# A list schedule ordered by one rank for each piece, in a block-sparse attention with a gated feed-forward layer

## The chip, the cores and the metric

The kernel runs on one core of one Trainium2 chip. The metric is the time of one execution on the device in microseconds (us), as the median of several runs. The core has five engines that run on their own and wait for each other by semaphores: TensorE (PE; PEld is its weight load), VectorE (DVE), ScalarE (ACT), GpSimd (POOL) and SyncE (SP). SP and POOL here also issue the transfers (DMAs): those of SP are on queue q1, those of POOL on queue q0.

## The reference

Attention of 4 batches, 8 heads, 768 positions in 24 blocks of 32, 64 wide, with a block mask; its output goes through a gated feed-forward layer ("expert" in the change's words; there is one).

```python
scores = scale * np.matmul(q, k.transpose(0, 1, 3, 2))
mask = np.abs(blk_i - blk_j) <= window          # the block itself and its two neighbours
mask = mask | (blk_i == 0) | (blk_j == 0) | (blk_i == n_blocks - 1) | (blk_j == n_blocks - 1)
for qb in range(n_blocks):
    for kb in sampled_blocks[qb]:               # three blocks given at run time
        mask[qb * block:(qb + 1) * block, kb * block:(kb + 1) * block] = True
attn = softmax(np.where(mask, scores, -1e9))
x = (attn @ v), heads side by side: (3072, 512)
gate = 1.0 / (1.0 + np.exp(-(x @ w_gate)))      # w_gate, w_val: (512, 1536)
out = (gate * (x @ w_val)) @ w_out              # w_out: (1536, 512)
```

## The kernel before

The kernel describes its work as about 1,100 pieces, each with a name, an engine (or a choice of two), an estimated duration, the pieces that it depends on, the buffers that it takes and gives back, and a priority. A planner (`Planner.run`, L197) then makes a list schedule when the kernel is built: again and again it takes, for each engine, among the pieces that could start soonest (within 0.2 us on TensorE, 0.02 on the others) the one with the lowest priority number, and appends it. The result is a fixed order of instructions on each engine. On the chip each engine works through its order, and an instruction that waits holds up all behind it.

The pieces of one batch b, by the start of their names:
- `ldv`, `ldk`, `ldq` (L559, L563): loads of V, K, Q with a cast to f16, on POOL's queue. The weights `wg`, `wv` in four quarters each and `wo` in three (L578, L586) are on the same queue. `GATES` (L37) lists weight loads that are let go only after a named V gather of batch 0 was issued, and `LGATE` (L40) does so for the loads of the next batch.
- `shk`, `shq` (L722): a rearrangement of the loaded K or Q in SBUF from heads to rows, on POOL or VectorE; `vsh` (L773) the same for V on VectorE, and `scr` (L782) writes it to DRAM.
- `trk`, `trq` (L743; L746 in batch 0): TensorE transposes, four for each; `evk`, `evq` (L756, L761, L763) take them out of PSUM to `KT` and `QT`, on VectorE or ScalarE.
- `kfl`, `kg` (L881, L870): gathers of the first, last and three sampled K blocks of a query block into `KG`, the latter on POOL.
- `w`, `vg` (L815, L894): gathers of V windows and sampled V blocks from DRAM, on SP. `vfl` (L799; L681 in batch 0) fetches V's first and last block to `FL`, and `vfc` (L827 on VectorE, L829 on POOL) copies them beside each window.
- For each of 11 steps of two query blocks: `sc` scores (L914, L921), `mx` row maximum (L930, VectorE), `ex` exponential (L942, ScalarE), `rz` reciprocal (L949), `sl` scaling (L965 on VectorE, L962 on ScalarE), `tp` transpose (L976, TensorE), `te` its copy (L982), `pv` product of P and V (L995), `xe` its copy to the layer's input `XA` (L1011, L1016). In batches 2 and 3 the scores of two steps are one piece.
- Four "dense" units for the first and last query block, which see all keys: `dsc` (L644), `dmx` (L1046), `dex` (L1052), `dsl` (L1060, L1061), `dtp` (L1070), `dte` (L1075), `dpv` (L1083), `dxe` (L1100).

The feed-forward layer works on seven groups of 256 or 512 positions (`GROUPS`), each of which can start when the attention of its positions is done. A group has 12 pieces, one for each 128 hidden columns: a gate half and a value half on TensorE (L1138, four matmuls each), a tanh on ScalarE (L1146) and a multiply on VectorE into `HT` (L1151). Then comes one output piece of 12 matmuls for each 128 positions (L1173), scaled into `YS` (L1180, L1182) and stored by SP (L1187). The output piece reads the 12 parts of `HT` in their order. While TensorE would stand in the first 60 us, the planner puts filler matmuls in (L1207).

What sets the order: attention pieces have a priority of 10 b plus 0.1 for each step, expert pieces 1000 + 100 g + f for part f of group g, so that attention goes first and expert pieces go by number. `OFFSETS` (L44) adds a small number for each kind of piece and batch, and for quarters of a batch (`kind`, L72; `third`, L83), in one loop before the planner runs (L1216 to L1218).

Of the kernel before, what the change touches and what calls it, by code (L numbers as in the profile page):

```python
# [33 lines left out]
PREP = [-50.0, 0.27, 10.34, 20.65]  # L34


GATES = {0: 4, 2: 7, 3: 7, 4: 9, 6: 5, 7: 7, 8: 6}  # L37


LGATE = {1: 10, 2: 11, 3: 2}  # L40

OFFSETS = {  # L44
    "dense1": 0.26, "dense2": 0.10, "dense3": 0.10, "evk0": -0.74, "evk1": -0.80, "evk2": -1.45, "evk3": -0.55,
    "evq0": 1.25, "evq1": 0.23, "evq2": -0.22, "evq3": -1.58, "ex0": 0.01, "ex0.d": -0.84, "ex1": -0.18,
    "ex1.b": -0.01, "ex1.c": -0.03, "ex1.d": 0.01, "ex2": -1.17, "ex2.c": 0.10, "ex3": -3.42, "ex3.a": -0.08,
    "ex3.d": -0.29, "kfl0": -0.91, "kfl1": -0.90, "kfl2": -0.39, "kfl3": -0.88, "kg0": -0.57, "kg0.a": 0.09,
    "kg1": 0.44, "kg1.d": 0.06, "kg2": 0.38, "kg3": 1.19, "kg3.c": 0.03, "ldk0": -0.43, "ldk1": -0.02, "ldk2": -0.35,
    "ldk3": 0.64, "ldq0": 0.85, "ldq1": 0.76, "ldq2": -0.07, "ldq3": -0.32, "ldv0": -0.29, "ldv1": 0.02,  # L50
    "ldv2": 0.03, "ldv3": -0.01, "mx0": -0.39, "mx1": 0.02, "mx1.c": -0.01, "mx2": 0.03, "mx3": 1.95, "mx3.d": 0.02,
    "pv0": 0.57, "pv1": 0.02, "pv1.b": 0.26, "pv1.c": 0.30, "pv1.d": 0.54, "pv2": -0.07, "pv2.a": 0.06, "pv3": 1.33,
    "pv3.c": -0.25, "rz0": -1.33, "rz0.b": 0.04, "rz0.c": 0.02, "rz1": 0.18, "rz1.b": -0.37, "rz1.d": 0.16,
    "rz2": -0.18, "rz2.c": 0.08, "rz2.d": -1.06, "rz3": -2.19, "rz3.a": 0.35, "rz3.c": -0.66, "sc0": -0.04,
    "sc0.c": 1.29, "sc0.d": 0.01, "sc1": -0.04, "sc1.a": 0.32, "sc2": -0.40, "sc2.b": 0.01, "sc3": 0.07,
    "sc3.a": 0.68, "scr0": 1.03, "scr1": 0.86, "scr2": -2.19, "scr3": 0.72, "shk1": 0.12, "shk2": -0.83,
    "shk3": 0.25, "shq1": 0.21, "shq2": 0.21, "shq3": 1.91, "sl0": -0.54, "sl0.c": 0.04, "sl1": -2.38, "sl2": -0.07,
    "sl2.a": 1.08, "sl2.c": -0.06, "sl2.d": -0.48, "sl3": 2.15, "te0": 0.19, "te0.a": 0.89, "te0.d": 0.03,
    "te1": 0.28, "te1.a": 0.82, "te1.b": 0.06, "te2": 0.03, "te3": -0.62, "te3.a": -0.57, "te3.c": -0.18,
    "tp0": 0.19, "tp0.a": -0.07, "tp1": -0.18, "tp1.c": 0.20, "tp1.d": 1.12, "tp2": 0.13, "tp2.d": -0.01,  # L60
    "tp3": 0.14, "tp3.b": 0.45, "trk0": -0.17, "trk1": 0.02, "trk2": -0.07, "trk3": -0.68, "trq0": -0.55,
    "trq1": -0.41, "trq2": -0.01, "trq3": 0.27, "vfc0": -0.46, "vfc1": -0.62, "vfc2": 0.03, "vfc3": -0.03,
    "vfl0": 1.61, "vfl1": -1.53, "vfl2": -0.18, "vfl3": 1.68, "vg0": -0.06, "vg1": -0.57, "vg1.d": 0.01, "vg2": 0.05,
    "vg3": 0.17, "vg3.b": 0.10, "vsh0": -0.45, "vsh1": 0.09, "vsh2": -0.22, "w0": 0.04, "w0.c": 1.86, "w1": -1.01,
    "w1.a": -0.04, "w1.d": -0.16, "w2": -0.63, "w2.c": 0.37, "w2.d": 0.08, "w3": 0.23, "w3.b": 0.03, "wg0": 0.97,
    "wg1": -0.05, "wg2": -0.51, "wg3": -0.04, "wo0": -0.07, "wo1": 0.62, "wo2": -0.30, "wv0": 0.24, "wv1": 1.00,
    "wv2": 0.32, "wv3": -1.88, "xe0": -0.31, "xe0.d": 0.33, "xe1": -1.46, "xe2": -0.10, "xe2.c": -0.61, "xe3": -0.01,
    "xe3.d": -0.01,
}


def kind(o):  # L72

    if o.prio <= -90 or o.prio >= 900:
        return None
    n = len(o.name) - len(o.name.lstrip("abcdefghijklmnopqrstuvwxyz"))
    c, b = o.name[:n] or "x", o.name.lstrip("abcdefghijklmnopqrstuvwxyzABCDEFGHIJKLMNOPQRSTUVWXYZ")[:1]
    if c in ("dsc", "dmx", "dex", "dsl", "dtp", "dte", "dpv", "dxe"):
        c = "dense"
    return c + (b if b.isdigit() else "x")  # L80


def third(o, k):  # L83

    n = o.name.split("_")
    x = n[1] if k is not None and len(n) > 1 and n[0].isalnum() and n[0][-1].isdigit() else ""
    d = x[: len(x) - len(x.lstrip("0123456789"))]
    return k + "." + "abcd"[min(int(d) // 6, 3)] if d and n[0][:-1].isalpha() else None


class Op:
# [264 lines left out]
def kernel(  # L356
# [145 lines left out]
    pl = Planner()  # L502
# [606 lines left out]
    for b in range(B):  # L1109
        lv = attention(b, 10.0 * b, prev)  # L1110
        for n, i in GATES.items() if b == 0 else ():
            FF["gate"][n].after.append(vgs[0, i])
        prev = [lv] + ([FF["w"]["wo", NF - 1]] if b == 0 else []) + ([vgs[b, LGATE[b + 1]]] if b < B - 1 else [])

# [6 lines left out]
    for g, G in enumerate(GROUPS):  # L1121
        n = 128 * len(G)
# [90 lines left out]
        return o  # L1213

    pl.fill = fill
    for o in pl.ops:  # L1216
        k = kind(o)
        o.prio += OFFSETS.get(k, 0.0) + OFFSETS.get(third(o, k), 0.0)  # L1218
    order = pl.run()
    PLAN.clear()  # L1220
    PLAN.extend((o.name, o.eng, o.start, o.end) for o in order)
# [36 lines left out]
```

## Time and profile before

| what | value |
|---|---|
| runs | 334.35 us median of 3 (333.45 to 334.68) |
| the profiled execution | 333.25 us; span from first to last instruction 331.5 us |
| mean granted TensorE clock | 0.995 |
| TensorE busy | 309.1 us (93%), of which fillers (L1207) 10.8 + 10.2 us |
| VectorE, ScalarE, POOL busy | 241.4, 219.1, 100.9 us |
| first expert matmul (L1138) | 44.6 us |
| q0: transfers of POOL | 16.39 MB |
| q1: transfers of SP | 24.83 MB |

A busy TensorE is not TensorE at its peak, as its matmuls overlap. Times of the order of work are from the start of the span. In the rows of a timeline stand start, length, engine, line, operation, what is written and read, how many instructions, and in brackets how long the engine stood before and what ended that. In the rows of stages stand the stage, its length, the busy time of PE, PEld, DVE, ACT and POOL with their instructions, the granted clock, the DMA share and GB/s.

### The profile page before, as it was taken

The numbers are of one execution on the slowest core, as the hardware profiler recorded it, in microseconds if no ns is written. First come the engines' busy times: TensorE is split into PE (matmuls) and PEld (weight loads), VectorE is DVE, ScalarE is ACT, GpSimd is POOL, SyncE is SP. The second block draws the span as 40 slices with busy tenths as digits, with TensorE's granted clock in tenths as the row PEclk, the third lists the DMA queues.
The fourth block names the chain that finished last, engine by engine and source line by source line (L and its number), as shares of the span: only waits on it lengthen the run. The fifth ranks groups of instructions, "written<-read, shape, count | busy, mean of one in ns | idle before, by whom it ended". The sixth has DMA issues, their size and how long they took to land.

```text
span 331.5 us, 12349 instructions
## 1 busy us (share of the span) xinstructions
PE 309.1 (93%) x4568; PEld 187.1 (56%) x4568; DVE 241.4 (73%) x542; ACT 219.1 (66%) x650; POOL 100.9 (30%) x332
## 2 busy tenths in 40 slices
PE   6998887998899799999999999999999999999996
PEld 2555566866766356655555655655655665444443
DVE  3399899936887979878898969999996577504310
ACT  1248889854597789766998566679995868423322
POOL 6499642036743632402330427022220010000000
PEclk9999999999999889999999999999999999999999
DMA  7959999979449862235389093531323400020002
GB/s 116 195 186 228 224 226 227 222 184 269 110 69 231 242 136 87 71 96 145 115 159 190 32 223 114 157 96 35 108 72 116 117 11 3 0 97 32 0 34 95
DMA packets 42063, 41.99 MB, mean 127 GB/s; under 512 B 6323, under 2 KB 38196, under 8 KB 42004
## 3 DMA queue, kind: packets, MB, share of 16 engines
q0 software_dynamic: 17376, 16.39, 30.0%
q1 hardware_dynamic: 24628, 24.83, 25.4%
q8 instruction: 36, 0.59, 0.8%
q14 instruction: 23, 0.19, 0.2%
HBM read 45.97 MB, written 9.44 MB: 167 GB/s over the span
## 4 chain that ended last, share of the span: by engine, by line
PE 62%; DVE 13%; DMA 9%; issue 5%; ACT 5%; SPq 3%; POOL 1%; POOLq 0%; DVEq 0%
PE bank L1138 30%; PE bank L1173 13%; DMA V<-scr 5%; PE bank L976 4%; PE bank L995 3%; ACT P L942 3%; DMA out_dram<-YS 2%; SPq L894 2%; PE twin L921 2%; DVE NM L930 2%; DVE V L827 2%; DVE HT L1151 2%; PE twin L1207 2%; DVE P L965 1%; DMA scr<-stg 1%
## 5 line engine op out<-in xcount | busy, mean ns | idle before, releaser
L942 ACT ACTIVATE P<-twin,NM 128x256 f16<-128x256 f32 x176 | 81.5, 484 | 16.0 <-DVE NM L930 15.6
L870 POOL COPY KG<-KT 128x64 f32 x264 | 51.1, 245 | 121.2 <-PE twin L921 121.0
L1138 PE MATMUL bank<-XA,wg 128*128 128x512 f16 (+1 forms) x336 | 77.0, 352 | 2.0 <-DVE HT L1151 1.1
L1138 PE MATMUL bank<-XA,wv 128*128 128x512 f16 (+1 forms) x336 | 76.3, 350 | 2.1 <-ACT TH L1146 1.0
L1151 DVE SCALAR_TENSOR_TENSOR HT<-TH,bank 128x512 f16<-128x512 f32 (+1 forms) x84 | 50.9, 608 | 33.9 <-PE bank L1138 29.4
L1173 PE MATMUL bank<-wo,HT 128*128 128x512 f16 (+1 forms) x300 | 65.0, 371 | 0.0
L1146 ACT ACTIVATE TH<-bank 128x512 f32<-128x512 f32 (+1 forms) x84 | 45.5, 543 | 27.6 <-PE bank L1138 24.8
L930 DVE TENSOR_REDUCE NM<-twin 128x4 f32<-128x1024 f32 x44 | 52.4, 1216 | 0.5 <-PE twin L921 0.2
L1138 PEld LDWEIGHTS <-wv 128*128 128x128 f16 x336 | 31.4, 98 | 28.6 <-issue 4.9
L1173 PEld LDWEIGHTS <-HT 128*128 128x128 f16 x300 | 28.5, 98 | 29.8 <-issue 0.3
L1138 PEld LDWEIGHTS <-wg 128*128 128x128 f16 x336 | 30.1, 98 | 22.9 <-issue 3.1
L942 ACT ACTIVATION_READ_ACCUMULATOR P<-twin,NM 128x1 f32 x176 | 38.0, 216 | 0.0
L965 DVE TENSOR_SCALAR P<-P,ZZ 128x256 f16<-128x256 f16 x138 | 35.6, 318 | 1.5
L995 PEld LDWEIGHTS <-V 128*128 128x128 f16 x704 | 26.0, 98 | 13.7 <-issue 6.2
L1182 ACT ACTIVATE YS<-bank 128x512 f32<-128x512 f32 (+1 forms) x16 | 9.1, 571 | 28.7 <-PE bank L1173 28.7
L976 PEld LDWEIGHTS <-P 128*128 128x128 f16 x352 | 22.3, 98 | 9.4 <-issue 1.8
L995 PE MATMUL bank<-PTS,V 128*128 128x64 f16 x528 | 22.0, 193 | 4.3 <-DVE PTS L982 1.8
L976 PE MATMUL bank<-ident,P 128*128 128x128 f16 x304 | 23.5, 219 | 0.8 <-DVE P L965 0.4
L982 DVE COPY PTS<-bank 128x1024 f16<-128x1024 f16 x23 | 15.7, 681 | 6.0 <-PE bank L976 6.0
L962 ACT ACTIVATE P<-P,ZZ 128x256 f16<-128x256 f16 x38 | 17.1, 503 | 3.0 <-DVE ZZ L949 2.9
L921 PE MATMUL twin<-KG,QT 64*32 64x160 f16 x704 | 19.0, 236 | 0.0
L982 ACT COPY PTS<-bank 128x1024 f16<-128x1024 f16 x15 | 15.2, 1010 | 5.7 <-PE bank L976 5.4
(85 smaller groups left out, 372.4 us busy)
## 6 DMA issues: line engine op xcount, KB each, us to landing
V<-scr SPq DMA_DIRECT2D x264, 32.0 KB, 3.0
out_dram<-YS SPq DMA_DIRECT2D x23, 256.0 KB, 2.1
V<-scr SPq DMA_DIRECT2D x14, 288.0 KB, 3.3
stg<-in_v_dram POOLq DMA_DIRECT2D x4, 768.0 KB, 9.1
stg<-in_k_dram POOLq DMA_DIRECT2D x3, 768.0 KB, 14.2
scr<-stg SPq DMA_DIRECT2D x3, 768.0 KB, 4.4
stg<-in_q_dram POOLq DMA_DIRECT2D x3, 768.0 KB, 7.5
V<-scr SPq DMA_DIRECT2D x6, 384.0 KB, 5.4
```

The lines of the kernel that those rows point to most:

```text
L870: pin(nc.gpsimd.tensor_copy(t[:, :, 1 + n], KW[r][:, :, bass.ds(vals[(i - i0) * 3 + n], BLK // 2)]))
L921: pin(nc.tensor.matmul(t[hh][cs, u, c0:c1], QT[r][rs, p, BLK * i : BLK * i + BLK], src, start=False, stop=True, skip_group_check=True))
L930: pin(nc.vector.tensor_reduce(NM[o.slots[hz][1]][:, 0:4], t, axis=AX.X, op=ALU.max, negate=True))
L942: pin(nc.scalar.activation(pb[:, u, :], t[:, u, :], AF.Exp, bias=NM[z][:, x : x + 1], scale=1.0, accum_out=ZZ[z][:, x : x + 1]))
L965: pin(nc.vector.tensor_scalar(pb[:, u, :], in0=pb[:, u, :], scalar1=ZZ[z][:, 2 * hh + u : 2 * hh + u + 1], scalar2=None, op0=ALU.mult))
L976: pin(nc.tensor.transpose(t[:, c * 128 : c * 128 + 128], pb[:, c * 128 : c * 128 + 128], ident))
L982: pin(copy(o)(PTS[pl.handles[hTS][1]].rearrange("k c q -> k (c q)"), banks[o.slots[hT][1]].bitcast(f16)))
L995: pin(nc.tensor.matmul(t[:, u, p, :], vt[:, ws, p * 128 : p * 128 + 128], pt[:, u, c, :, 32 * p : 32 * p + 32], start=(c == 0), stop=(c == ...
L1138: pin(nc.tensor.matmul(t, wt[:, c, f_ * 128 : f_ * 128 + 128], XT[g][:, c, :], start=(c == 0), stop=(c == 3)))
L1146: pin(nc.scalar.activation(TH[o.slots[ht][1]][:, 0:n], banks[o.slots[hg][1]][:, 0:n], AF.Tanh, bias=0.0, scale=0.5))
L1151: pin(nc.vector.scalar_tensor_tensor(HT[:, f_, hoff : hoff + n], in0=TH[o.slots[ht][1]][:, 0:n], scalar=1.0, in1=banks[o.slots[hv][1]][:, ...
L1173: pin(nc.tensor.matmul(t, HT[:, f_, hoff + tt * 128 : hoff + tt * 128 + 128], wo[:, f_, cols], start=(f_ == 0), stop=(f_ == NF - 1)))
```

## The change

The offsets and the two functions that name a piece's kind go. In their place stands a list of ranks, one for each piece in the order in which the pieces are made, and the loop sets each priority to its rank. Attention and expert pieces share one scale. The gates of the loads are other ones. Nothing else differs: pieces, durations, buffers, fillers and the planner are the same.

```diff
-GATES = {0: 4, 2: 7, 3: 7, 4: 9, 6: 5, 7: 7, 8: 6}
-LGATE = {1: 10, 2: 11, 3: 2}
-OFFSETS = {
-    "dense1": 0.26, "dense2": 0.10, "dense3": 0.10, "evk0": -0.74, "evk1": -0.80, "evk2": -1.45, "evk3": -0.55,
...
-}
-def kind(o):
...
-def third(o, k):
...
+GATES = {6: 5, 7: 8, 10: 9}
+LGATE = {1: 18, 2: 13, 3: 13}
+RANKS = [
+    530, 262, 525, 261, 260, 297, 294, 268, 296, 284, 283, 301, 347, 304, 288, 287, 366, 303, 357, 372, 326, 642,
...
+    1366, 1042, 57, 1370, 952, 77, 1372, 951, 52, 1371, 1040, 74,
+]
...
-    for o in pl.ops:
-        k = kind(o)
-        o.prio += OFFSETS.get(k, 0.0) + OFFSETS.get(third(o, k), 0.0)
+    for o, rank in zip(pl.ops, RANKS, strict=True):
+        o.prio = rank
     order = pl.run()
```

In the orders that the two programs have, expert parts of a group no longer go by number (group 0: 4, 5, 1, 2, 11, 9, 8, 7, 10, 3, 6, 0; the last group ends with part 3). On TensorE the transposes of K of batch 1 come after five pieces of group 1 instead of after one and an output piece, and those of K of batch 2 after four pieces of group 2 instead of one and a half. The last attention piece of batch 3 stands ahead of the last output piece of group 5, instead of ahead of its first. On POOL the rearrangement `shq` of batch 1 stands behind a fill `vfc` instead of ahead of two, and that of batch 2 behind four gathers `kg`. On SP the fetch `vfl` of batch 1 stands ahead of the first output store instead of behind it.

## The prediction

> **What bounds the kernel now.** I read the page first, then TensorE's waits, then stages of 10 us, then the order of time on TensorE and POOL. The page's parts 1 and 2 (a digit is a fortieth of the span, 8.3 us):
>
> ```profile
> PE 309.1 (93%) x4568; PEld 187.1 (56%) x4568; DVE 241.4 (73%) x542; ACT 219.1 (66%) x650; POOL 100.9 (30%) x332
> PE   6998887998899799999999999999999999999996
> PEclk9999999999999889999999999999999999999999
> ```
>
> TensorE (PE) is the bound: from slice 17 on it is never under 9 tenths. What can still be saved is its idle time, 22.4 us in all (331.5 - 309.1), and the half-speed stretch that PEclk shows in slices 14 and 15. The stages, with PE's busy time first after the stage's length:
>
> ```profile
> 50.00:60.00 10.00, 7.71 (x144) 6.53 (x141) 9.11 (x27) 9.55 (x33) 1.62 (x9) 1.00 1.23 228
> 80.00:90.00 10.00, 7.83 (x157) 6.38 (x156) 9.54 (x15) 3.93 (x12) 8.79 (x20) 1.00 0.71 168
> 110.00:120.00 10.00, 7.83 (x93) 4.13 (x92) 8.80 (x20) 7.15 (x22) 4.92 (x14) 0.83 0.94 222
> 230.00:240.00 10.00, 10.00 (x173) 5.96 (x172) 9.71 (x24) 9.43 (x33) 2.19 (x12) 1.00 0.35 96
> ```
>
> The holes lie ahead of 120 us. Before 60 us VectorE and ScalarE are 91 to 96% busy and the DMA share is over 1, so PE there waits for them and for V. The two single holes that matter, and the POOL work that sets them:
>
> ```profile
> 72.15 0.51 PE L743 MATMUL bank<-ident,stg 96*128 96x96 f16 x8
> 82.51 0.60 PE L1138 MATMUL bank<-XA,wg 128*128 128x256 f16 x4 [1.13 <-DVE HT L1151]
> 105.48 1.02 PE L1138 MATMUL bank<-XA,wg 128*128 128x512 f16 x4 [0.38 <-DVE XA L1011]
> 112.90 0.51 PE L743 MATMUL bank<-ident,stg 96*128 96x96 f16 x8 [2.17 <-POOL stg L722]
> ```
>
> ```profile
> 69.15 1.89 POOL L722 COPY stg<-stg 96x2048 f32<-96x2048 f32 x1 [12.28 <-DMA stg<-in_k_dram]
> 70.99 0.78 POOL L563 DMA_DIRECT2D stg<-in_q_dram  x1
> 78.07 1.66 POOL L870 COPY KG<-KT 128x64 f32 x9
> 79.67 1.90 POOL L722 COPY stg<-stg 96x2048 f32<-96x2048 f32 x1
> 82.16 4.50 POOL L829 COPY V<-FL 32x768 f32<-32x768 f32 x4
> 110.95 1.89 POOL L722 COPY stg<-stg 96x2048 f32<-96x2048 f32 x1 [2.31 <-DVE PTS L982]
> ```
>
> L722 rearranges a batch's K or Q after its load; PE's L743 transposes need it. At 112.90 PE had stood 2.17 us for the one of K of batch 2 (its load landed at 110.79). Right behind, at 114.3, the granted clock fell to 0.5 for 3.41 us: 0.83 in that stage, so 1.7 us of work lost. The hole costs 3.87 in all. Two shorter ones, 1.16 and 1.13 us near 51, brought no such fall. The Trainium skill (TensorE: Matmul & The Clock Gate, "Why this matters for your kernels") asks for no idle gaps over about 3 us to keep the clock; by that rule the hole would cost 2.17 alone. The row decides: here 2.17, with smaller pauses just ahead of it, was enough.
>
> **The change, part by part.** Work is the same instruction for instruction in kind (4,568 matmuls, 76 of them fillers, in both), so no duration changes; only order, the choice of VectorE or ScalarE for some copies, and when loads are let go. I went through both orders engine by engine and counted what stands ahead of four places.
>
> 1. *Start to K transposes of batch 1 (72.15).* Ahead of the first of them stand, before, 12 pieces of expert group 0, one of group 1 and one 12-matmul output piece, which is as long as three (2.6 against 3 x 0.87): 16 pieces. After: 11 of group 0 and 5 of group 1, again 16, and the attention pieces are the same (11 transposes and 9 products of batch 0, all 4 dense units). So this stretch gives only what K's arrival lets it: 69.04 landing, 1.89 rearranged, end 71.04, so 71.2 instead of 72.15. The load queue carries the same bytes in front of that load (it never ran empty from 20 to 69 us), so it lands no earlier. Value -0.95. It needs the first expert piece to come no later than now (44.57); its fourth product of P and V has gone ahead of a transpose whose copy it waited for (0.67), so I expect about 1 us sooner, and the weights' third and fourth quarters (landed 44.84 and 50.26) are needed at about 47 and 50: zero to 0.8 lost, hidden by the wait for K. Three gates hold weight loads instead of seven, and the second value quarter now stands on POOL behind eight more gathers of K, some 3 us later (issued 28.66 now, landed 40.30); the queue still has 7 us of transfers ahead of it then, so its landing stays. If this cover is gone it shows at 71.2.
>
> 2. *To the first scores of batch 1 (86.84).* From 71.2 PE has 8 transposes of batch 1 (4 of 0.34 twice: 2.7), pieces (0.87 each) 4, two output pieces 5.2, two products 1.0: 12.4, so 83.6 if nothing waits. The chain is K rearranged 71.04, Q loaded (78.22 now), Q rearranged (1.9), transposes, evacuation, scores. Now Q's L722 starts at 79.67, 1.45 after the landing, behind POOL's gathers L870, and from its end (81.57) to the scores 5.27 pass, with PE held 1.13 and 0.57 by VectorE. After, the evacuations are two on each of VectorE and ScalarE (0.55 and 0.82) instead of three on one: 3.4 instead of 5.27. But the moved POOL queue has Q's L722 behind a V fill (L829, two copies of 1.0 = 2.0), which needs the FL rows: they landed at 79.64 and 79.95, having been issued behind an output store and a register load; the new SP order drops the store ahead of them, and the copy that feeds scr stands ahead of fewer VectorE pieces, so I take 78.3. Then L722 runs 80.3 to 82.2 and the scores come at 85.6: -1.25. Ends: no wait for the fill, 78.2+1.9+3.4 = 83.5, PE-bound 83.6: -3.2. FL as late as now: 79.95+2.0+1.9+3.4 = 87.3: +0.5.
>
> 3. *To the first piece of expert group 2 (105.48).* 18.6 us of VectorE and ScalarE chain for four attention steps; unchanged in kind, so group 2 starts at 104.2. But one score piece (0.51) and one transpose piece (0.45) more are done by then, which come off the rest: -0.95 (the 16 + 20 = 36 pieces of expert work ahead are equal). I do not count item 1 again: its gain is inside 85.6.
>
> 4. *The hole at 110.73.* PE now reaches the transposes after 3 expert halves; after, behind 8 halves of 0.865 (four 128x512 matmuls), one score, one transpose, two products, a dense score and two dense transposes: 6.92 + 3.05 = 10.0, so at 114.2. The K load of batch 2 is let go later (from 96.59 to about 102, behind four more gathers, L870, that wait for scores), but it moves only after V (landed 103.34) and took 7.4 from there: 111 to 112.4, rearranged by 112.9 to 114.3. The hole is 0 to 0.4 and below where the clock fell. Value -3.0 (ends -3.87 and 0).
>
> 5. *The rest.* From 120 on PE has 1.87 us of single waits left (0.30, 0.68, 0.33, 0.56). Reordered pieces will have others: +1.0 (ends -1 and +3). Attention now reaches to the last output piece of group 5 instead of ending four pieces earlier; VectorE was 57% busy at 250 to 270, so it is free there.
>
> 6. *The end.* The last hidden piece is now number 3 of 12, which the output piece reads at its fourth matmul (0.65 in) instead of its twelfth: the multiply on VectorE (0.68) and TensorE's drain make it ready about 1.0 after the last matmul: +0.3 (0 to 0.6).
>
> On POOL, L722 and VectorE's scaling L965 collided at 111: four copies took 2.65 instead of 0.88. The Trainium skill (SBUF — State Buffer, "Who interferes with whom") says the later of two such instructions blocks for the whole of the first. By that rule the same 1.8 us comes back wherever L722 meets a scaling, in either order. The trace agrees at that row; the sum leaves it as it is.
>
> Sum: -1.25 - 0.95 - 3.0 + 1.0 + 0.3 = -3.9. The profiled execution took 333.25 (span 331.5 and 1.75 around it); the median of three, 334.35, is 1.1 above it. I forecast on the median: 334.35 - 3.9 = 330.4.
>
> **The rivals.**
> *A, all holes go.* Items 2 and 4 at their best ends, nothing new in the rest: -3.2 - 0.95 - 3.87 + 0 + 0.3 = -7.7: 326.6. For it: the late stages already run at 10.00 of 10. Against: 1,100 pieces in a new order with no new wait.
> *B, no change.* The order is new, but K's landing (69.04) and the VectorE chain of 18.6 set the middle; the hole at K of batch 2 stays a hole (over 2 us, with the clock), because its load went later by 5: -1.25 - 0.95 + 0 + 2 + 0.3 = +0.1: 334.4. For it: that load took 14.2 us from issue. Against: 10.0 of work now stands ahead of the transposes.
> *C, slower: Q of batch 1 rearranged behind the fill.* PE reaches Q's transposes at 71.2 + 9.75 = 80.95 (K transposes 1.4, two and a half pieces, two output pieces, two products). With FL at 79.95, L722 ends at 83.85: PE stands 2.9 us, and as after the 2.17 the clock halves, 1.7 more: 4.6 where this stretch now idles 2.14 (0.44, 1.13, 0.57): +2.5; the later load of K then costs its 0.4 in full, rest and end +1.3, and the hole at 112 is replaced, not removed, as group 2 starts later: 334.35 + 2.5 + 0.4 + 1.3 - 0.95 = 337.6. It decides when FL lands after about 79.2 (80.95 + 2.14 - 1.9 - 2.0). For it: now it lands at 79.95. Against: less stands ahead of its issue.
>
> **How the numbers follow.** Forecast 0.42 (its own range 328.5 to 332.6); A 0.15; B 0.16; C and its like 0.27. This measurement can tell 0.5% (1.7 us) from no change. Faster holds the forecast and A, 0.57; the same 0.16; slower 0.27. The range 327 to 338 reaches from A to C and leaves out the tails beyond each.
>
> **What would show it.** Right: no wait for L722 over 1 us on TensorE, no stretch of clock 0.5 after 20 us, batch 1's first scores before 86.5, group 2's first piece before 105. Item 1 is wrong if K's transposes begin after 72.2; item 2 if Q's L722 starts after 81; item 4 if PE again waits over 2 us near 112. The forecast fails if PE's idle time after 120 us is above 5 us, or if the clock halves twice.

## The result, and the profile after

The changed kernel took 335.13 us (median of 20 runs, 332.37 to 338.68) beside 333.38 us for the kernel before (20 runs): a ratio of 1.0055, with a 95% interval of 1.0032 to 1.0079. It is slower by about half a per cent where the forecast had 330.4 us, 3.9 under the median of three runs that it started from. Here and below, ratios and mean clocks leave out executions more than 1.5% above the fastest of their kernel; medians are of all. Its profiled execution took 334.16 us, with a span of 332.4 us (before: 333.25 and 331.5), so it is one of its shorter ones.

Lines of the changed kernel are those of the kernel before plus 22. First its page, busy times and the 40 slices:

```profile
PE 305.8 (92%) x4568; PEld 185.9 (56%) x4568; DVE 244.9 (74%) x545; ACT 216.4 (65%) x654; POOL 100.0 (30%) x325
PE   6898589899787999999969999999999999999986
PEclk9999989999999999999999999999999999999999
```

The dip in PEclk at slices 14 and 15 is gone, as forecast, but a new one stands in slice 6 (the half clock is at 40.0 to 43.4 us), and PE's lowest digits are in slices 5 (33 to 42 us) and 21 (166 to 175 us). TensorE's waits, with what ended them (time in total, how often, the longest):

```profile
PE twin L943 <- issue: 2.6, 2, 2.3
PE bank L1017 <- issue: 2.4, 1, 2.4
...
PE bank L765 <- POOL stg L744: 1.1, 1, 1.1
PE bank L1195 <- DVE HT L1173: 0.8, 1, 0.8
```

The two longest behind the start have no releaser: "issue" means that nothing which the profile shows held the engine. The same places in order of time, with the milestones that the forecast named:

```profile
40.28 0.48 PE L1017 MATMUL bank<-PTS,V 128*128 128x64 f16 x6 [2.42 <-issue]
73.09 0.51 PE L765 MATMUL bank<-ident,stg 96*128 96x96 f16 x8
84.11 0.51 PE L765 MATMUL bank<-ident,stg 96*128 96x96 f16 x8 [1.06 <-POOL stg L744]
87.31 0.28 PE L936 MATMUL twin<-mrow,ones 64*32 64x192 bf16 x8
109.23 1.02 PE L1160 MATMUL bank<-XA,wg 128*128 128x512 f16 x4 [0.46 <-DVE XA L1033]
120.50 0.51 PE L765 MATMUL bank<-ident,stg 96*128 96x96 f16 x8
174.36 0.26 PE L943 MATMUL twin<-KG,QT 64*32 64x160 f16 x8 [2.28 <-issue]
318.57 0.81 PE L1195 MATMUL bank<-wo,HT 128*128 128x512 f16 x3 [0.85 <-DVE HT L1173]
```

K of batch 1 is transposed at 73.09, its first scores come at 87.31, group 2's first piece at 109.23, K of batch 2 at 120.50 without a wait. Two stages, with PE's busy time behind the length of the stage:

```profile
110.00:120.00 10.00, 9.23 (x136) 5.29 (x134) 9.61 (x22) 7.23 (x18) 3.23 (x5) 1.00 0.91 206
170.00:180.00 10.00, 7.72 (x169) 4.97 (x167) 5.95 (x9) 5.34 (x15) 2.69 (x13) 1.00 1.04 209
```

From 110 to 120 us PE is busy 9.23 at full clock, where it was 7.83 at 0.83. From 170 to 180 us, where the kernel before had no wait, it stands 2.28 us in the middle of one score step, between two matmuls of the same kind.

To see where time is lost in a profile, each piece of TensorE can be counted with its own length (the rows' pitch: 0.44 or 0.87 us for an expert half, 2.59 for an output, 0.35 for a transpose of K or Q, and so on; fillers count nothing). The time less the work done by then is what has been lost; the total is 274.3 us in every kernel. The second column is another profile of the kernel before (e7 below), the last two are kernels from the experiments.

| lost by, us | before | before, again | changed | e6 | e17 |
|---|---|---|---|---|---|
| 50 us | 31.6 | 31.5 | 33.6 | 30.7 | 30.8 |
| 90 | 39.5 | 39.5 | 38.7 | 38.1 | 37.0 |
| 110 | 42.8 | 43.5 | 44.5 | 43.2 | 41.5 |
| 120 | 46.8 | 45.7 | 45.9 | 45.2 | 42.8 |
| 170 | 49.2 | 48.4 | 48.4 | 47.1 | 48.3 |
| 180 | 49.5 | 48.6 | 50.9 | 48.8 | 48.8 |
| 310 | 53.7 | 53.3 | 53.6 | 52.2 | 53.3 |
| 320 | 53.7 | 53.3 | 54.6 | 52.2 | 53.3 |

The changed kernel is 2 us behind at 50 us, gets ahead by 0.8 until 90, loses 5.8 from 90 to 110 (before: 3.3, and 4.0 in its second profile), gains 2.6 where the hole was (0.8 beside the second profile), loses 2.5 from 170 to 180 (before: 0.3) and 1.0 at the end (before: none).

### The profile page after: what moved, and what is told of

The parts are those of the page before. It is cut to its first block, busy times and chain, and to the rows that moved or that the text cites. A ratio compares the mean times of both kernels' runs of the same rounds, so it can differ in the third digit from the quotient of the medians.

```text
span 332.4 us, 12247 instructions
## 1 busy us (share of the span) xinstructions
PE 305.8 (92%) x4568; PEld 185.9 (56%) x4568; DVE 244.9 (74%) x545; ACT 216.4 (65%) x654; POOL 100.0 (30%) x325
## 4 chain that ended last, share of the span: by engine, by line
PE 62%; DVE 14%; ACT 12%; issue 5%; DMA 4%; POOL 2%; DVEq 0%; ACTq 0%; POOLq 0%
PE bank L1160 26%; PE bank L1195 17%; ACT P L964 8%; DMA stg<-in_q_dram 4%; PE bank L998 3%; DVE NM L952 3%; PE bank L1017 3%; PE twin L943 2%; DVE HT L1173 2%; DVE P L987 2%; PE twin L1017 1%; ACT PTS L1004 1%; PE twin L936 1%; PE bank L765 1%; PE twin L998 1%
## 5 line engine op out<-in xcount | busy, mean ns | idle before, releaser
L1160 PE MATMUL bank<-XA,wg 128*128 128x512 f16 (+1 forms) x336 | 75.1, 349 | 1.0 <-DVE HT L1173 0.6
L1160 PE MATMUL bank<-XA,wv 128*128 128x512 f16 (+1 forms) x332 | 74.2, 348 | 1.2 <-ACT TH L1168 0.6
L1173 DVE SCALAR_TENSOR_TENSOR HT<-TH,bank 128x512 f16<-128x512 f32 (+1 forms) x83 | 49.7, 607 | 27.5 <-PE bank L1160 23.3
L1160 PEld LDWEIGHTS <-wv 128*128 128x128 f16 x336 | 31.5, 98 | 27.0 <-issue 1.9
L1017 PEld LDWEIGHTS <-V 128*128 128x128 f16 x704 | 25.3, 98 | 13.5 <-issue 5.8
L998 PEld LDWEIGHTS <-P 128*128 128x128 f16 x352 | 22.7, 99 | 9.5 <-issue 2.7
L1017 PE MATMUL bank<-PTS,V 128*128 128x64 f16 x464 | 18.8, 194 | 3.3 <-issue 2.4
L998 PE MATMUL bank<-ident,P 128*128 128x128 f16 x272 | 20.8, 219 | 0.6 <-DVE P L987 0.3
L744 POOL COPY stg<-stg 96x2048 f32<-96x2048 f32 x6 | 11.5, 1912 | 31.9 <-DVE stg L795 12.1
L1004 ACT COPY PTS<-bank 128x1024 f16<-128x1024 f16 x13 | 13.2, 1017 | 11.0 <-PE bank L998 11.0
L849 DVE COPY V<-FL 32x2048 f16<-32x2048 f16 (+1 forms) x20 | 16.7, 883 | 3.6 <-DMA FL<-scr 2.8
```

What stands on the lines that cost most here:

```text
L849: pin(nc.vector.tensor_copy(dst, src.broadcast_to([BLK, n, DM])))
L998: pin(nc.tensor.transpose(t[:, c * 128 : c * 128 + 128], pb[:, c * 128 : c * 128 + 128], ident))
L1017: pin(nc.tensor.matmul(t[:, u, p, :], vt[:, ws, p * 128 : p * 128 + 128], pt[:, u, c, :, 32 * p : 32 * p + 32], start=(c == 0), stop=(c == ...
L1160: pin(nc.tensor.matmul(t, wt[:, c, f_ * 128 : f_ * 128 + 128], XT[g][:, c, :], start=(c == 0), stop=(c == 3)))
L1173: pin(nc.vector.scalar_tensor_tensor(HT[:, f_, hoff : hoff + n], in0=TH[o.slots[ht][1]][:, 0:n], scalar=1.0, in1=banks[o.slots[hv][1]][:, ...
```

## The experiments

The medians, and the ratio to the kernel before run beside them; the clock is the mean over the executions of the mean granted TensorE clock. The ratio is not that of the medians of this column (beside e6 the kernel before had 332.97), so kernels of different rows are compared by their ratios first.

| run | us | ratio, 95% interval | clock |
|---|---|---|---|
| changed | 335.13 | 1.0055 (1.0032 to 1.0079) | 0.989 |
| e1 changed, again | 335.37 | 1.0103 (1.0041 to 1.0164) | 0.988 |
| e2 parts in order of issue | 334.89 | 1.0064 (1.0026 to 1.0103) | 0.991 |
| e3 shift by 64 places | 333.56 | 0.9998 (0.9964 to 1.0033) | 0.996 |
| e4 before, K transposes later | 333.04 | 1.0009 (0.9973 to 1.0045) | 0.997 |
| e5 other bank at the end | 334.49 | 1.0039 (1.0005 to 1.0073) | 0.990 |
| e6 shift, bank, order of issue | 332.03 | 1.0001 (0.9964 to 1.0039) | 0.993 |
| e7 before, again | 332.26 | 0.9995 (0.9963 to 1.0027) | 0.997 |
| e8 before, shift by 168 | 335.69 | 1.0095 (1.0062 to 1.0129) | 0.991 |
| e9 load let go later | 335.80 | 1.0055 (1.0022 to 1.0088) | 0.988 |
| e10 before, shift by 20 | 333.54 | 1.0006 (0.9977 to 1.0034) | 0.996 |
| e12 e6 and a third bank | 332.26 | 0.9969 (0.9937 to 1.0002) | 0.996 |
| e13 Q ahead of the fill | 336.11 | 1.0085 (1.0049 to 1.0120) | 0.984 |
| e14 e6 and Q ahead | 333.94 | 1.0010 (0.9978 to 1.0042) | 0.993 |
| e15 e12 and Q ahead | 332.65 | 0.9987 (0.9958 to 1.0015) | 0.995 |
| e16 e14, one fill to POOL | 332.43 | 0.9961 (0.9929 to 0.9992) | 0.996 |
| e17 e14, two fills to POOL | 330.85 | 0.9929 (0.9895 to 0.9963) | 0.997 |
| e18 e17 and a third bank | 331.61 | 0.9960 (0.9925 to 0.9994) | 0.997 |

The kernel before has a mean clock of 0.995 in the executions beside e1 to e4.

**What has no releaser.** Counted in the programs, every instruction of TensorE has a place in its stream (matmuls, weight loads and waits; 9,240 before, 9,212 after). The page lists 36 packets of 16 KB on a queue named "instruction" (9,212 places are 36 blocks of 256), and the gaps without a releaser of over 1 us in both first profiles stand at places 1730 (before), 1218 and 5570 (after), all 194 more than a multiple of 256, with such a packet starting 2.2 to 2.4 us ahead of the gap's end. That is theory F: at the end of a block of its instructions TensorE stands until the next block has been fetched. The queues around the gap at 172.08 us, first from the end of the block before it (166.3) to 171.9, then from 171.9 to the gap's end:

```profile
q0 software_dynamic: 905, 0.70, 97.3%
q1 hardware_dynamic: 194, 0.25, 14.8%
```

```profile
q0 software_dynamic: 378, 0.34, 83.0%
q1 hardware_dynamic: 278, 0.23, 37.1%
q8 instruction: 1, 0.02, 2.3%
```

The load of batch 3 holds 97.3% of the time of the 16 transfer engines for 5.6 us, and no instruction packet goes; it goes at 172.0, and TensorE runs on 2.4 us later. The block itself lasted only 5.8 us.

e1, the changed kernel again:

> The changed kernel once more, nothing edited. Theory F (instruction fetch): the gaps of TensorE that have no releaser stand again at the same places of its instruction stream, 1218 (2.4 us, near 38 to 40 us) and 5570 (2.3 us, near 172 us), whatever the run; a stray stall of the chip would be elsewhere or gone. Theory S (spread): the run's median is again about 1 us over its first profile, 334.7 to 335.6 us against 333.0 to 333.8 for the kernel before, and its executions with a mean clock of 0.983 to 0.985 are 1 to 2 us longer than those with 0.99 to 0.995; if clock and time don't go together, the spread has another cause.

```profile
40.13 0.34 PE L1017 MATMUL bank<-PTS,V 128*128 128x64 f16 x6 [2.40 <-issue]
174.45 0.26 PE L943 MATMUL twin<-KG,QT 64*32 64x160 f16 x8 [1.42 <-issue]
```

Both gaps are at places 1218 and 5570 again. Over all twenty profiles, 31 of the 33 gaps without a releaser (over 0.2 us, after 14 us) stand at 194 or 195 past a multiple of 256; the two others, 0.8 us each, are one and the same matmul at 175 us in e6 and e18. The clock half of the expectation: the median was 335.37, but clock and time go together only loosely in single executions (0.995 with 335.2, 0.979 with 338.7; over 25 executions of the changed kernel 0.01 less clock goes with 1.7 us more, with a correlation of -0.53).

e3, the shift:

```diff
         def f(o):
             for x in range(n):
-                pin(nc.tensor.matmul(banks[y[1]]...512 columns
+                h = 2 if t0 < 4.0 or 8.0 < t0 < 10.0 else 1
+                for z in range(h):
+                    pin(nc.tensor.matmul(banks[y[1]]...512 // h columns
```

> The changed kernel with 32 of the filler matmuls before 15 us cut into two of half the width: the same work in the same order, but every later instruction of TensorE stands 64 places further on in its stream. Theory F: no gap without a releaser at 172 us, since the fetch of that block is now asked for about 2 us before the load on the input queue starts; the median falls by 1.5 to 2.5 us against the changed kernel, to 332.5 to 333.6 us; the gap near 38 us moves or goes, worth 0 to 1.5 us more or less, because that stage waits for weights anyway. Rival: what stalls at 172 us is the piece itself (its operands, its bank), not its place in the stream; then the gap of 2.3 us stays with that piece and the median stays within 0.5 us. Second rival: the gap goes and the later stages, held by ACT and DVE, take the time back: median within 0.5 us with no gap.

No gap without a releaser is left in its profile, neither at 38 nor at 172 us. The median is 333.56, 1.6 to 1.8 us under the two changed runs, and the ratio to the kernel before falls from 1.0055 and 1.0103 to 0.9998. Same work, same order: theory F holds, and its price is about the whole loss (the interval reaches from 0.9964 to 1.0033). e8 does the opposite to the kernel before:

```diff
+                h = 4 if 6.0 < t0 < 10.0 else 1
```

> The kernel before with its filler matmuls between 6 and 10 us planned time cut into four of a quarter of the width: the same work in the same order, every later instruction of TensorE 168 places further on. Theory F says that this alone makes it slower: by the trace of before, block ends then fall at 104.6 and 109.5 us, with their fetches asked for while the two loads of batch 2 run (97.3 to 110.3 us), for gaps of about 1.6 and 3.3 us, the second partly in place of the 2.17 us that is lost there now; and up to 3 us more before 65 us, partly under the waits for weights. Together 2 to 5 us: 335 to 338 us. Rival: the place in the stream matters only by chance of one execution; then it stays within 0.7 us of the kernel before.

```profile
20.26 0.32 PE L921 MATMUL twin<-KG,QT 64*32 64x160 f16 x3 [1.85 <-issue]
36.64 0.26 PE L921 MATMUL twin<-KG,QT 64*32 64x160 f16 x6 [1.75 <-issue]
```

It is 0.95% slower, by the shift alone. But of the places that I had named the early ones came, which I had thought half hidden, and of those at 104 and 110 us only 0.25 us (the fetches came just in time). When a fetch is late I can't foretell to 2 us from one trace. e10 says so too:

```diff
+                h = 2 if t0 < 4.0 else 1
```

> The kernel before with the first ten filler matmuls cut into two of half the width: 20 places further on in TensorE's stream. Theory F: by the trace of before, the gap at 52.5 us (1.1 us) moves away or shrinks under 0.4 us; whether the one near 108 us (0.2 us in one profile, 1.7 us in the next) goes is open, as a load runs on either side of it. Median 0.3 to 1.5 us under the kernel before. Rival: the stage before 65 us waits for weights whatever TensorE does; then within 0.3 us.

```profile
54.21 0.52 PE L995 MATMUL bank<-PTS,V 128*128 128x64 f16 x12 [1.44 <-issue]
```

The gap did not shrink (1.44 instead of 1.13): it stayed at place 1731 of the stream and so moved to another matmul, and one of 1.57 us stood at place 3522. The time is that of the kernel before. e9 was to move the load instead of the stream:

```diff
-LGATE = {1: 18, 2: 13, 3: 13}
+LGATE = {1: 18, 2: 13, 3: 17}
```

> The changed kernel with every engine's order and TensorE's stream as they are; only the loads of batch 3 (V and K) wait for the gather of step 17 instead of that of step 13, which should start them 2 to 3 us later than 166.4 us. Theory F: the fetch asked for at 166.3 us (end of block 5314) then goes out within 1 us, as it is ahead of the load, and the gap at 172 us goes, though nothing moved in the stream; the gap near 38 us stays with its clock. Median 0.8 to 2.0 us under the changed kernel (334.5 to 335.4 us). Rival: the load's place has nothing to do with it; the gap stays at 2.3 to 2.8 us. Third outcome: the gap goes, but K of batch 3 is late and TensorE waits for its transposes near 185 us instead.

It settles nothing: the load's packets still started at about 167.4 us, as in e1, right after the block's end at 167.3, and the gap stayed (2.78 us). That the load is what makes the fetch late is so far read from traces only.

**The end.** In e2 the outputs of the last group add up the parts in the order of issue (`sorted(range(NF), key=lambda f_: hs[f_].end)`).

> The changed kernel with one edit: the outputs of the last group add up the twelve parts in the order in which the ranks issue them, instead of 0 to 11, so that part 3, issued last, is also used last. Theory T (tail): the wait of 0.85 us for DVE's HT ahead of the first output at 317.7 us shrinks to under 0.2 us, and the median falls by 0.6 to 0.9 us against the changed kernel. Rival: the wait only moves into the outputs, as DVE is as late with part 3 as before; then the median falls by less than 0.3 us.

The wait stayed at 0.85 us, on the first matmul. So it does not wait for part 3 as an operand. In the program this matmul writes bank 5, which the last value half had taken and the last multiply on HT sets free. e5 keeps the outputs off that bank:

```diff
-                      count=NF, acq=[(hy, pg_of(g))])
+                      count=NF, acq=[(hy, [x for x in pg_of(g) if g < len(GROUPS) - 1 or x != ("bank", 5)])])
```

> The changed kernel; the outputs of the last group no longer use bank 5, into which the last half piece (pv6_3) writes, so that the first output starts in bank 6, free since an earlier piece. Theory T2 (bank): in the run with the parts in issue order the wait stood ahead of the first matmul, though the part that this one reads was long done; what it waits for is the bank, set free by the last DVE instruction on HT. Then the wait of 0.85 us ahead of the first output goes to under 0.15 us, a wait of 0.1 to 0.3 us for part 3 may remain inside the output, and the time falls by 0.5 to 0.8 us. Rival: TensorE waits for the whole of HT there, whatever the bank; then 0.85 us stays.

The wait is gone, so it was the bank. The median is 0.64 us under the changed kernel's 335.13, a difference that the intervals of the two ratios do not separate. e6 joins e3, e5 and e2:

> The changed kernel with the shift of 64 places in TensorE's stream, the other bank for the outputs of the last group, and its parts added up in the order of issue. Theories F and T2 together: no gap without a releaser over 0.5 us, no wait over 0.2 us at the last outputs, median 1.6 us (the shift) and 0.8 us (the bank) under the changed kernel: 332.4 to 333.1 us, level with the kernel before or up to 0.3% under it. If the two gains overlap or are taken back by ACT and DVE, it stays at 333.4 to 334 us.

```profile
316.16 5.13 PE L1196 MATMUL bank<-wo,HT 128*128 128x512 f16 x23
```

The first output follows without a wait. 332.03 us is 3.1 under the changed kernel by the medians; by the ratios (1.0055 to 1.0001) it is 1.8, no more than e3 gains alone, and level with the kernel before. What the bank is worth in time is not shown.

**The hole.** e4, e9 and e12 to e18 replay the planned orders of all engines from a list, with single pieces moved; their lines are 9 more than in the kernel before, 13 less than in the changed one. e4 is the kernel before with

```diff
-PE: ... pg2_1, trk200, pv2_1, sc1_2, trk210, pg2_2, pv2_2 ...
+PE: ... pg2_1, pv2_1, sc1_2, pg2_2, trk200, trk210, pv2_2 ...
```

> The kernel before, every engine's order as it was, but for four pieces on TensorE: the first transpose of batch 2's K stands behind two expert half pieces and one score step (pv2_1, sc1_2, pg2_2) instead of ahead of them. This is the one gain that the forecast had counted on (the hole of 2.17 us at 110.7 us and the half clock behind it, 1.7 us), without the rest of the change. If the hole is worth its length: no idle over 0.5 us there, no half clock at 112 to 118 us, and a median 3.0 to 3.9 us under the kernel before (about 329.5 to 330.5 us). Rival G (given back): DVE is busy 4.9 of 5.0 us from 105 to 115 us and ACT's exponentials wait for it, so that TensorE waits elsewhere before 130 us; then 0 to 1.5 us are left of it.

```profile
111.32 0.44 PE L985 MATMUL bank<-ident,P 128*128 128x128 f16 x5 [1.61 <-issue]
...
116.85 0.50 PE L752 MATMUL bank<-ident,stg 96*128 96x96 f16 x8 [0.93 <-ACT KT L765]
```

The wait of 2.17 us for POOL is gone and the clock never fell, yet the time is that of the kernel before. A gap for instructions (place 3522) and a wait for ScalarE took its place. The second profile of the kernel before shows why:

> The kernel before once more, nothing edited, for the clock of each of its executions and a second profile. Theory S: its executions show a mean clock of 0.990 to 1.0, more than those of the changed kernel (0.983 to 0.995), as its longest idle time of TensorE is 2.2 us in one place against 2.3 to 2.8 us in two. If its clocks are the same as those of the changed kernel, the half clock explains none of the difference between them.

```profile
110.00 0.44 PE L976 MATMUL bank<-ident,P 128*128 128x128 f16 x5 [1.67 <-issue]
```

There K's transposes do not wait at all (busy 10.00 of 10 from 110 to 120 us); the instruction gap of 1.67 us stands ahead of them, with the half clock behind it. The hole that I had read was one of two faces of this place. As for the clock, 0.997 here against 0.988 and 0.989 is what the expectation said.

**The stage from first scores to group 2.** It took 18.64 us in the first profile of the kernel before, and 18.64 or 18.65 in e4, e7, e8 and e10; in the changed kernel 21.92, and 21.92 or 21.93 in nine of eleven other profiles with its order (22.1 in e1, 22.7 in e14). In it stand seven score steps and five transposes instead of six and four, and eight expert halves instead of ten: 0.08 us more of work (0.51 + 0.45 - 2 x 0.44), but 4.12 us of waits instead of 1.28. e11 takes load off ScalarE there; it leaves out most of the softmax of two steps:

```diff
-pin(nc.scalar.activation(pb[:, u, :], t[:, u, :], AF.Exp, ...
+w = 16 if b == 1 and st[0] in (14, 18) else 256
+pin(nc.scalar.activation(pb[:, u, 0:w], t[:, u, 0:w], AF.Exp, ...
```

> The changed kernel, but the exponentials of two steps of batch 1 (14 and 18) are taken of 16 of 256 columns: this leaves out most of the softmax of these two steps and takes some 0.9 us for each off ACT, with every order as it was. Theory A (the stage from 87 to 109 us is set by ACT, on which the exponentials of step 14 stand ahead of what the first pieces of expert group 2 need): the time from the first scores of batch 1 to the first piece of group 2, 21.9 us in the changed kernel, falls by 0.9 to 2 us, and the waits of TensorE for ACT's P and XA between 94 and 108 us shrink. Rival: DVE's own chain (maxima, scaling) sets it; then it falls by less than 0.4 us.

TensorE's waits in that stage of e11 (lines one more than in the changed kernel):

```profile
PE bank L1018 <- ACT XA L1034: 0.8, 1, 0.8
PE twin L999 <- ACT P L965: 0.8, 1, 0.8
PE bank L1161 <- ACT TH L1169: 0.6, 1, 0.6
PE bank L1161 <- DVE HT L1174: 0.6, 1, 0.6
```

The stage stayed at 21.92 us (one profile, 335.25 us): the load of these exponentials is not what sets it. The four waits shown, and a fifth of 0.5 us, are, by the program, of matmuls that write a bank or twin of PSUM which an earlier piece still holds; the name behind the arrow is that of its last reader. e12 gives the transposes a third one, on top of e6:

```diff
-    ptpool = bk(4, 3)
+    ptpool = bk(4, 7, 3)
```

> The kernel of e6_shift_bank with every engine's order as it was, and a third PSUM bank (7) that the transposes of attention's P may take ahead of bank 3, which they share with the scores. In e6_shift_bank, as in every profile of the changed kernel, the first piece of expert group 2 starts 21.93 us after the first scores of batch 1 (18.64 us in every profile of the kernel before). Theory P (PSUM): of the seven waits in that stage five end with a bank set free; those of 0.82 us (a transpose behind exponentials that still hold bank 3) and 0.35 us go, the stage shortens by 0.7 to 1.3 us, to 20.6 to 21.2 us, and the median falls by up to 1 us under e6_shift_bank (332.0 us). Rival: the order itself sets the stage, with two outputs of 2.59 us ahead of the last transposes; then it stays at 21.7 to 22.1 us, the waits only move, and the median stays within 0.5 us. It may also be longer than e6_shift_bank by up to 1 us where the experts miss bank 7.

(The planner also puts in four more fillers, 8 places.) The stage fell to 20.94 us (21.2 in e18, 21.5 in e15) and the wait of 0.82 went. The time stayed (332.26 to e6's 332.03): of the 3.3 us that the stage had grown, 0.4 to 1.0 hung on this shortage of PSUM; what holds the rest is not shown. It brought no time: that profile lost 3.1 us at the Q transposes, ahead of the stage, and e18 with that wait mended is no faster than e17.

**The Q transposes.** e13 puts `shq1` ahead of `vfc13` on POOL.

> The changed kernel with one edit on POOL's queue: the rearrangement of batch 1's Q (shq1) stands ahead of the fill of V buffer 3 (vfc13) instead of behind it. The forecast's rival C named this place. In the changed kernel Q lands at 79.3 us, the fill runs from 79.6 to 82.1 us, and TensorE waits 1.1 us at 83.1 us for the rearrangement behind it. Theory C: the rearrangement starts when Q lands, 2.5 us or more sooner, the wait goes to under 0.3 us, the first scores of batch 1 come 1.0 to 1.5 us sooner (from 87.3 to 85.8 to 86.3 us where the gap near 38 us stays), and the median falls by 0.8 to 1.5 us under the changed kernel (335.1 to 335.8 us). Rival: DVE, busy 5.0 of 5.0 us there, is late with the evacuations of Q, or the stage that follows takes it back; then within 0.4 us.

```profile
77.67 1.89 POOL L731 COPY stg<-stg 96x2048 f32<-96x2048 f32 x1 [1.22 <-DMA stg<-in_q_dram]
```

```profile
77.80 6.48 DVE L836 COPY V<-FL 32x2048 f16<-32x2048 f16 x6 [3.22 <-DMA FL<-scr]
84.31 0.56 DVE L770 TENSOR_SCALAR QT<-twin 128x768 f16<-128x768 f16 x1
```

```profile
84.92 0.50 PE L752 MATMUL twin<-ident,stg 96*128 96x96 f16 x8 [2.73 <-DVE QT L770]
```

Q is rearranged as soon as it lands, and TensorE waits longer, for an evacuation on DVE behind three fills in a row. The time did not fall (336.11). Theory C had the place; with it mended the next holder stands there. e14 and e15 add the edit to e6 and e12, and gain nothing either:

> The edit of e13_q_first together with those of e6_shift_bank (64 places, other bank for the last outputs, parts in order of issue). If the terms add up: e6_shift_bank's 332.0 us less 1.0 to 1.8 us (its wait at the Q transposes is 1.8 us): 330.2 to 331.0 us, 0.5 to 0.9% under the kernel before with an interval that leaves out 1. If the stage from 87 to 120 us takes it back: 331.6 to 332.3 us.

> The same with the third bank for the transposes of P (e12_third_bank). If those terms add up too: 329.8 to 331.0 us, and the stage from first scores to group 2 again 20.9 to 21.0 us. The wait of 3.1 us at the Q transposes in the profile of e12_third_bank goes.

The last three take fills off DVE (e16 one, e17 two, e18 two and the third bank); the orders of e17 beside those of e6:

```diff
-POOL: ... vfc13, shq1, kg1_11 ...        DVE: ... vfc10, vfc11, vfc12, evq130 ...
+POOL: ... shq1, vfc13, vfc11, vfc12, kg1_11 ...        DVE: ... vfc10, evq130 ...
```

> e14_q_first_shift_bank with one of DVE's three fills of batch 1's V buffers (vfc12) moved to POOL, behind shq1 and vfc13. e13 and e14 showed that with Q rearranged in time TensorE still waits, 2.7 and 3.4 us, for an evacuation of Q on DVE that stands behind three fills in a row (6.5 us from 77.8 us in e13). Theory D (the fills on DVE): two fills are left ahead of the evacuation, it starts about 2 us sooner, and the wait falls to 0.5 to 1.5 us; median 331.0 to 332.3 us (e6_shift_bank had 332.0 us, e14 333.9 us). Rival: DVE is the bound of the whole stage from 78 to 100 us, so that later pieces wait by as much; then the median stays at 332.5 to 334 us.

> The same with two of DVE's fills (vfc11 and vfc12) on POOL: one fill is left ahead of the evacuation. Theory D: no wait over 0.4 us at the Q transposes, first scores of batch 1 at 83.5 to 84.5 us, median 330.2 to 331.5 us. Rival: POOL's four gathers behind the fills come late for the next scores (planned 0.7 us later), or DVE bounds the stage anyway; then 331.5 to 333 us.

> e17_two_fills_moved with the third bank for the transposes of P (e12_third_bank). If the terms add up, the lowest of all: 329.8 to 331.2 us, with an interval against the kernel before that leaves out 1. If the stage takes them back: 331.5 to 333 us.

The rows of DVE and of TensorE in e17:

```profile
78.31 3.53 DVE L836 COPY V<-FL 32x2048 f16<-32x2048 f16 x2 [2.88 <-DMA FL<-scr]
81.98 0.56 DVE L770 TENSOR_SCALAR QT<-twin 128x768 f16<-128x768 f16 x1
```

```profile
82.53 0.50 PE L752 MATMUL bank<-ident,stg 96*128 96x96 f16 x8 [0.22 <-ACT QT L772]
82.87 0.50 PE L752 MATMUL twin<-ident,stg 96*128 96x96 f16 x8
84.18 0.28 PE L923 MATMUL twin<-mrow,ones 64*32 64x192 bf16 x8
```

The evacuation starts 3.3 us sooner than in the changed kernel (85.24), where three fills (5.71 us) stood ahead; the wait is 0.22 and the first scores come at 84.18. e14 and e17 differ in two fills alone: 333.94 and 330.85 us, and 1.0010 and 0.9929 by the ratio. e17 is the fastest kernel here, 0.7% under the kernel before (7 executions) with an interval that leaves out 1; e16 and e18 also are. e18 was to be lower still and is not (331.61): the third bank adds nothing again. The profile of e17 is of its slowest execution (332.90 us). There a later wait takes back what was won, for the evacuation of batch 2's Q:

```profile
134.51 0.28 PE L923 MATMUL twin<-mrow,ones 64*32 64x192 bf16 x8 [2.47 <-DVE QT L770]
```

## Why the forecast was wrong

The milestones, from the rows of TensorE (us):

| | forecast | before | changed | e6 | e17 |
|---|---|---|---|---|---|
| K transposes of batch 1 | 71.2 | 72.15 | 73.09 | 71.05 | 71.23 |
| first scores of batch 1 | 85.6 | 86.84 | 87.31 | 85.98 | 84.18 |
| first piece of group 2 | 104.2 | 105.48 | 109.23 | 107.91 | 106.10 |
| K transposes of batch 2 | 114.2, no hole | 112.90 | 120.50 | 119.83 | 117.42 |

*The missing term: TensorE's own instructions.* None of the steps and none of the rivals had it. The gap of 1.13 us near 51 was in the profile that I quoted, and I named it a short pause that brought no clock fall, without asking what it waited for; a row without a releaser is a question. The change moves every piece to another place in the stream and two block ends into dense score and product steps while the loads run. e3 gives the price, 1.6 to 1.8 us. Part of it is the clock: 0.9886 in the mean is (1 - 0.9886) x 2 x 332 = 7.6 us at half speed in an execution, against 3.3 us for the kernel before (0.9951), which is 2.2 us of work at most; at the 1.7 us for 0.01 of e1's paragraph the difference is worth 1.1 us. How the price divides between standing and clock is not shown.

*1, K of batch 1:* argued rightly, 71.05 in e6; 73.09 in the changed kernel, past the bound of 72.2 that I had set, because the gap of 2.42 us at 37.9 and the half clock behind it (40 to 43.4 us) eat the "about 1 us sooner" of the expert pieces (46.75 instead of 44.57; 44.05 and K at 71.25 in e3, the shift alone).

*2, first scores:* argued rightly too. Without the gaps, in e6, the fill starts when FL lands, Q's rearrangement follows it, and the scores come at 85.98:

```profile
78.30 2.48 POOL L851 COPY V<-FL 32x768 f32<-32x768 f32 x2 [1.24 <-DMA FL<-scr]
80.84 1.89 POOL L744 COPY stg<-stg 96x2048 f32<-96x2048 f32 x1
82.78 0.51 PE L765 MATMUL bank<-ident,stg 96*128 96x96 f16 x8 [1.82 <-POOL stg L744]
```

The forecast had 78.3, 80.3 and 85.6. In the changed kernel all of it comes 1.3 us later: the fill at 79.63, the rearrangement at 82.17 (my bound was 81), the scores at 87.31. What I had not counted are the three fills on VectorE behind it, which e13 brought out.

*3, a step that failed in every profile: "18.6 us of VectorE and ScalarE chain for four attention steps; unchanged in kind".* It is 21.92. I compared kinds and counts of work ahead, and added the extra score and transpose (0.95 us) as a gain; with one more score step and one more transpose in the stage, TensorE waits 2.84 us longer, five of its seven waits being for PSUM buffers that are still held. Only 0.4 to 1.0 us of it went with a third buffer, so the cause of the rest stays open.

*4, the hole:* right as to the place (no wait, full clock, 120.50), wrong as to the price. 3.0 us came from one execution's row; in another the hole is not there, and e4 shows that without it the kernel before is not faster (1.0009, 0.9973 to 1.0045, so at most 0.9 us faster). A hole is worth its length only if nothing else is due at that place.

*5, the rest:* from 120 to 310 us 7.7 us were lost instead of 6.9, so +0.8 for my +1.0 (+0.1 beside the second profile of the kernel before); but 2.3 of it is the block end at 172 us, and without that the rest is a gain of 1.5 to 2.2. That +1.0 was near is luck.

*6, the end:* 0.85 instead of 0.3, and for the bank, not for part 3.

*The rivals:* B's time (334.4) was nearest, but its reason, the hole staying, was false. C's place was there with 1.06 us (1.82 in e6) instead of 2.9, and not as the main cost. Of the signs of being right none held: a wait of 1.06 us for the rearrangement, half clock at 40.0 us, and both milestones late.

Together: the forecast was 3.9 us of gain and the result 1.75 of loss. Of the 5.6 us between them 1.6 to 1.8 are the block ends (e3) and 2.1 to 3.0 the price of the hole (e4); the rest, 0.9 to 1.9 us, no run divides among the stage of step 3 and the others. Without the gaps and the wait at the end the change is level with the kernel before (e6); with three pieces of POOL and VectorE moved as well it is 0.7% faster (e17).

## What to carry to other kernels

Before pricing a new order, list every wait that has no releaser and find its place in the instruction stream: in a kernel with thousands of small matmuls a reorder moves block ends as well as work, and a few instructions more at the start can be worth as much as the reorder. A hole read in one profile should be looked for in a second one before it is counted as a gain. Where a stage holds one more step of the same kind, count what the step holds (banks, one engine's queue), not only how long it is.

## What the runs showed of the hardware

*Instruction blocks.* TensorE's instructions come in packets of 16 KB for 256 places. In the first profiles of both kernels, after 70 us, the packet started 2.0 to 6.1 us after the block end before it in nine cases, all with a load of POOL's queue not yet landed, and at most 1.7 us after it otherwise; where TensorE stood, it used the new block 2.2 to 2.4 us after the packet's start. The blocks that ended in a gap there had lasted 5.2 to 5.9 us, so only dense blocks under a load show one, up to 3.6 us (e13, place 5570). That the load is the cause is read from the traces; e9 was to test it and did not move the load. The Trainium skill (Runtime: NRT & Kernel Launch, "Instruction fetch mechanics") has the blocks of 256 and calls the cost of a boundary mostly hidden; the blocks agree, and here a boundary cost 0.8 to 3.6 us in the worst places, which is not hidden.

*The clock.* In each profile all stretches of half clock lie on a grid of 3.413 us. In the twenty profiles, 16 windows of that grid between 14 and 325 us hold 1.9 us or more without a matmul, and all 16 are followed by a half-clock window; of 13 with 1.6 to 1.9 us, 5 are; of all the others three, two of them already at half clock (1.0 us in e16, 0.8 in e14) and one not (0.71 us, at 14.4 us in e12). So a gap of 2.3 us costs 1.7 us more (half of 3.413) or not, by where it falls on the grid: at 172 us it lay across two windows in the changed kernel's first profile (no fall) and inside one in e2 (fall). The Trainium skill (TensorE: Matmul & The Clock Gate, "What's actually happening") gives the window of 3,413 ns and that it runs free, which agrees. The idle time of about 3 us that the Trainium skill asks to stay under (same page, "Why this matters for your kernels") is more than the runs bear out: 1.9 us within one window was enough every time.
